# Normalised attention followed by a gated MLP: the first group in halves, the g product on GpSimd, and a newly searched plan

## The chip, the cores and the metric

The kernel runs on one core of a Trainium2 chip. The metric is the device time of one execution in microseconds (us); the kernel is run several times and the median counts. One more execution is recorded by the hardware profiler, and the views quoted below come from that one.

## The reference

The attention part normalises every row of q and k by its root mean square and multiplies it by g_q or g_k, takes a softmax, and multiplies by v. The MLP part takes the 12 heads side by side as rows of 768, applies a first matrix with a relu, normalises one half (v) over its 512 columns, mixes that half along the sequence with w_spatial, multiplies by the other half (u), and applies the last matrix.

```python
# q, k, v: (8, 12, 448, 64) float32; g_q, g_k: (64,)
q_n, k_n = x / sqrt(mean(x * x, -1) + 1e-6) * g   # for q with g_q, for k with g_k
attn = softmax(q_n @ k_n.T / sqrt(64))
x = (attn @ v) with the heads side by side         # (8, 448, 768)
h = relu(x @ w_in)                                 # w_in (768, 1024)
u, v = h[..., :512], h[..., 512:]
v_n = (v - mean(v)) / sqrt(var(v) + 1e-6)
gated = u * (w_spatial @ v_n + b_spatial)          # w_spatial (448, 448), along the sequence
out = gated @ w_out                                # w_out (512, 768)
```

## The kernel before

The work is cut into 24 groups G of four heads, three groups to each of the 8 batches b. For a group the program loads q and k (448 KB each, 128 partitions x 2 x 448 float32, two heads on each half of the middle axis), squares them (line 498 on ScalarE, line 500 on VectorE or GpSimd), reduces the squares to one number per row (513), turns that into 1/rms with a logarithm and an exponential on ScalarE (520, 524), scales the rows to bf16 (537), and turns the result so that the head dimension lies on the partitions. For the first six groups TensorE turns it (553) and VectorE or ScalarE copies it out of PSUM (562, 564, 566); later groups use a transposing DMA on the SP queue (575). The product g_q * g_k / 8, a column called `g2_col`, is multiplied into k in that copy. It comes from two small loads (357), a product of two rows on VectorE (401), a one-column matmul (408) and a copy (412).

A group then has seven rounds: four matmuls of scores (604, 64 x 64 tiles, two at a time in the array) and one exponential over 128 x 896 on ScalarE (628). The sums of the exponentials (652, a matmul with ones) and the values (676) follow, with a reciprocal by logarithm and exponential (660, 664) and the product with it (685). After three groups a batch has its x, and the MLP of that batch follows: the v half (718, 722), relu (693, 695), its statistics (742, 746), logarithm and exponential (752, 756) and application (764), the u half (776), the spatial mix (792) with the gating product (797), and the output matmuls (816, 837) with their copies (804, 806) and stores (828, 848).

None of this is written in loops that run on the chip. Every step is a `Task` with an estimated cost on each engine that could do it, a due position `pos`, its dependencies, and the buffers that it takes (`get`) or holds (`use`). `Planner.run` lays the tasks out on the five engines one by one in estimated time, picking by position, and emits each task's instructions as it is placed. Several tasks can go to more than one engine. The result is a fixed order of instructions on every engine; each engine runs its own list in order, and semaphores connect the lists. A dependency may be written as a pair (task, early), which lets the planner start the dependent that much before the estimated end of the task. The table `NUDGE` holds some hundreds of corrections to positions and engine choices, found by a search against the planner's own estimates.

Four more pieces matter here. The four TensorE modes "S", "V", "G" and "O" stand for shapes of the array, and the planner counts 0.095 us for each change of mode. `fill` puts dummy matmuls (371) into gaps of TensorE up to 25.5 us of planned time. `hold_back` ties a load to a compute instruction that ends about when the load should start. `hand_over` makes GpSimd wait for the VectorE instruction[...].

```python
    LOOK = {"PE": 0.3, "ACT": 0.9, "DVE": 1.1, "POOL": 0.6, "SP": 0.2}
    WAIT = 4.0
    SWITCH = 0.095
    KEEP = 0.6
```

## Time and profile before

| what | value |
|---|---|
| median of 5 runs | 279.21 us (275.97, 276.42, 279.21, 279.99, 281.34) |
| the profiled execution, its own time | 279.84 us |
| its span, first to last instruction | 277.9 us |
| TensorE (PE) busy | 261.4 us, 94% |
| ScalarE (ACT) busy | 216.6 us, 78% |
| VectorE (DVE) busy | 201.1 us, 72% |
| GpSimd (POOL) busy | 158.7 us, 57% |
| TensorE clock granted, mean | 0.985 |
| HBM read and written | 38.55 MB and 11.01 MB |

The span starts at the first instruction of any engine, and the time of an execution also has what lies around the span, here 279.84 - 277.9 = 1.9 us. The page gives for every group of instructions its line, engine, tiles, count and mean duration in ns. Two views give order in time: the timeline (start, duration, engine, line, and in brackets the idle time before it with what ended it) and the chain of waits that ended last, followed back from the last instruction. Ends of matmuls are modelled by the profiler, so "busy" on TensorE also holds part of the pipeline's fill.

### The profile page before, as it was taken

The page shows a single profiled execution, that of the slowest core. Times are in us where ns is not written, and L with a number is a line of the kernel's source. Part 1 is how long each engine was busy: PE and PEld are TensorE (multiplying, and loading weights), DVE is VectorE, ACT ScalarE, POOL GpSimd, SP SyncE. Part 2 cuts the span into 40 slices and gives each one's busy share as a digit, 9 for nine tenths or more (in the row PEclk, how much of TensorE's full clock was granted, in tenths as well). Part 3 has the DMA queues.
Part 4 walks back from the last instruction along what each step waited for, and adds up shares of the span by engine and source line. Part 5 has one row for each costly group of instructions (what it writes and reads, how often), then busy time and mean ns, then how long its engine had stood idle before and what let it go on. Part 6 is the DMA issues. An engine that isn't in the chain of part 4 may idle for free.

```text
span 277.9 us, 7116 instructions
## 1 busy us (share of the span) xinstructions
PE 261.4 (94%) x2850; PEld 126.8 (46%) x2859; DVE 201.1 (72%) x350; ACT 216.6 (78%) x353; POOL 158.7 (57%) x130
## 2 busy tenths in 40 slices
PE   5669899999999999999999999999999999999991
PEld 5434464444344354444544454544444444455440
DVE  4686899977888559887786868877887667554760
ACT  4387999978889889787898788869889877994321
POOL 7556274079788795998597874876987340000000
PEclk9978999999999999999999999999999999999998
DMA  7989669589799989999999989977899491015006
GB/s 246 286 190 232 158 152 241 159 186 192 189 256 226 159 226 220 251 178 222 286 139 231 198 219 250 213 189 163 268 216 120 92 207 36 0 28 160 15 19 180
DMA packets 65506, 50.01 MB, mean 180 GB/s; under 512 B 41985, under 2 KB 61954, under 8 KB 65474
## 3 DMA queue, kind: packets, MB, share of 16 engines
q1 hardware_dynamic: 51266, 40.61, 59.9%
q0 software_dynamic: 13888, 8.27, 22.4%
q10 hardware_dynamic: 320, 0.69, 0.7%
q8 instruction: 22, 0.36, 0.5%
q14 instruction: 10, 0.08, 0.1%
HBM read 38.55 MB, written 11.01 MB: 178 GB/s over the span
## 4 chain that ended last, share of the span: by engine, by line
PE 79%; ACT 6%; DMA 5%; DVE 2%; POOL 2%; issue 2%; SPq 1%; ACTq 0%
PE ps L776 13%; PE ps L676 12%; PE ps L604 12%; PE ps L718 11%; PE ps L816 10%; PE ps L792 8%; PE ps L652 7%; ACT et L628 5%; DMA qf<-in_q_dram 4%; PE ps L722 2%; PE ps L837 2%; DMA out_dram<-osb 1%; PE ps L553 1%; PE ps L463 1%; POOL sq L500 1%
## 5 line engine op out<-in xcount | busy, mean ns | idle before, releaser
L628 ACT ACTIVATE et<-ps 128x896 bf16<-128x896 f32 x168 | 144.8, 917 | 21.5 <-PE ps L604 20.9
L513 DVE TENSOR_REDUCE ms<-sq 128x14 f32<-128x896 f32 (+1 forms) x50 | 51.3, 1039 | 7.2 <-POOL sq L500 6.0
L604 PE MATMUL ps<-qT,kT 64*64 64x448 bf16 x672 | 47.4, 363 | 4.7 <-ACT et L628 3.8
L685 DVE TENSOR_TENSOR xt<-ps,rc 128x448 bf16<-128x448 f32 x48 | 28.3, 620 | 21.6 <-ACT rc L664 13.3
L500 POOL TENSOR_TENSOR sq<-kf 128x896 f32<-128x896 f32 x23 | 38.6, 1680 | 7.3 <-DVE nk L537 3.0
L676 PE MATMUL ps<-et,vt 128*32 128x448 bf16 x768 | 42.0, 354 | 0.0
L500 POOL TENSOR_TENSOR sq<-qf 128x896 f32<-128x896 f32 x19 | 32.0, 1683 | 14.4 <-issue 5.0
L776 PE MATMUL ps<-xt,w_in 128*128 128x448 bf16 x192 | 40.1, 353 | 0.0
L537 POOL TENSOR_TENSOR nq<-qf,rs 128x896 bf16<-128x896 f32 x18 | 30.5, 1692 | 12.3 <-issue 6.3
L537 POOL TENSOR_TENSOR nk<-kf,rs 128x896 bf16<-128x896 f32 x18 | 30.5, 1692 | 8.4 <-ACT rs L524 5.7
L816 PE MATMUL ps<-w_out,gt 128*128 128x384 bf16 x192 | 34.2, 327 | 0.2 <-DVE gt L797 0.2
L718 PE MATMUL ps<-w_in,xt 128*128 128x512 bf16 x135 | 33.4, 380 | 0.8 <-issue 0.3
L426 POOL DMA_DIRECT2D vt<-in_v_dram x32 | 21.6, 680 | 16.6 <-DVE us L695 7.7
L604 PEld LDWEIGHTS <-kT 64*64 64x64 bf16 x672 | 16.4, 105 | 30.7 <-issue 26.4
L676 PEld LDWEIGHTS <-vt 128*32 128x32 bf16 x768 | 19.7, 96 | 18.5 <-issue 6.1
L792 PE MATMUL ps<-w_spT,vn 128*128 128x448 bf16 (+1 forms) x128 | 27.0, 353 | 0.1
L776 PEld LDWEIGHTS <-w_in 128*128 128x128 bf16 x192 | 17.2, 98 | 20.8 <-issue 6.6
L797 DVE TENSOR_TENSOR gt<-ps,us 128x448 bf16<-128x448 f32 x32 | 19.5, 621 | 8.2 <-PE ps L792 7.0
L816 PEld LDWEIGHTS <-gt 128*128 128x128 bf16 x192 | 17.5, 98 | 15.9 <-issue 4.9
L742 DVE BATCH_NORM_STATS2 s<-vs 128x6 f32<-128x512 bf16 (+1 forms) x32 | 21.6, 685 | 4.0 <-ACT vs L693 3.6
L652 PE MATMUL ps<-et,ones 128*32 128x448 bf16 x384 | 23.7, 364 | 0.0
L804 ACT ACTIVATE osb<-ps 128x384 f32<-128x384 f32 x31 | 14.6, 491 | 11.2 <-PE ps L816 8.4
(68 smaller groups left out, 260.4 us busy)
## 6 DMA issues: line engine op xcount, KB each, us to landing
qf<-in_q_dram SPq DMA_DIRECT2D x24, 448.0 KB, 4.6
kf<-in_k_dram SPq DMA_DIRECT2D x24, 448.0 KB, 4.5
out_dram<-osb SPq DMA_DIRECT2D x45, 192.0 KB, 3.1
vt<-in_v_dram POOLq DMA_DIRECT2D x16, 192.0 KB, 6.2
vt<-in_v_dram POOLq DMA_DIRECT2D x16, 144.0 KB, 6.1
w_in<-in_moe_w_in_dram POOLq DMA_DIRECT2D x2, 768.0 KB, 7.5
out_dram<-osb SPq DMA_DIRECT2D x15, 96.0 KB, 3.6
w_out<-in_moe_w_out_dram POOLq DMA_DIRECT2D x1, 768.0 KB, 9.7
```

The lines of the kernel that those rows point to most:

```text
L500: eng_of[e].tensor_tensor(out=sqb.t[:, h], in0=r.t[:, h], in1=r.t[:, h], op=ALU.mult)
L513: dve.tensor_reduce(out=ms.t[:, i, h], in_=sqb.t[:, h].rearrange("p a (s d) -> p a s d", d=D), axis=AX.X, op=ALU.add)
L537: eng_of[e].tensor_tensor(out=nb.t.rearrange("p s a d -> p a s d")[:, :, s0:s1, :], in0=r.t.rearrange("p a (s d) -> p a s d", d=D)[:, :, s ...
L604: pe.matmul(out=ps[64 * h:64 * h + 64, a, 0:S], lhsT=kb[64 * a:64 * a + 64, slot, 64 * xk:64 * xk + 64], rhs=qb[64 * a:64 * a + 64, :, 64 ...
L628: act.activation(out=eb.t[:, r], in_=bf.t[:, :, 0:S], func=AF.Exp, bias=0.0, scale=1.0)
L652: pe.matmul(out=bf.t[32 * l:32 * l + 32, 0:S], lhsT=ones[:, (0 if c < 3 else 1 + x), :], rhs=eb.t[:, r, a, :], start=(c == 0), stop=(c == ...
L676: pe.matmul(out=bf.t[32 * l:32 * l + 32, 0:S], lhsT=vb.t[:, 2 * (g + 3 * a) + x, c, half::2], rhs=eb.t[:, r, a, :], start=(c == 0), stop=( ...
L685: dve.tensor_tensor(out=xb.t[:, j * S:j * S + S], in0=bf.t[:, 0:S], in1=rc.t, op=ALU.mult)
L718: pe.matmul(out=bf.t, lhsT=xb.t[:, j * S + 128 * c:j * S + 128 * c + 128], rhs=w_in[:, j, DH:DF], start=(j == 0), stop=(j == 5))
L776: pe.matmul(out=bf.t[:, 0:S], lhsT=w_in[:, j, 128 * f:128 * f + 128], rhs=xb.t[:, j * S:j * S + S], start=(j == 0), stop=(j == 5))
L792: pe.matmul(out=bf.t[:, 0:S], lhsT=vn.t[0:kp, c, 128 * f:128 * f + 128], rhs=w_spT[0:kp, c, :], start=(c == 0), stop=(c == 3))
L816: pe.matmul(out=bf.t[:, 0:384], lhsT=gt.t[:, f, 128 * c:128 * c + 128], rhs=w_out[:, f, 384 * h:384 * h + 384], start=(f == 0), stop=(f == 3))
```

## The change

Four things change.

- The first loads are cut. q and k of group 0 come in two DMAs each, one for each half of the middle axis, and each square waits for its own half. The logarithm and exponential of group 0 are done for q and for k apart, so the scaling of q waits for q's sums alone. Later groups keep one load and one pair.
- The product of the g rows becomes a plain product that may run on VectorE or GpSimd (it lands on GpSimd), and the factor 1/8 moves into the copy of the column, which may run on ScalarE (it does) or VectorE.
- In the planner, a sums, values or v-half matmul group that continues another one no longer waits for the estimated 0.26 us until that one's result is out: the dependency becomes (task, 0.26).
- The table `NUDGE` is replaced as a whole; it was searched in two stages. With it the order of the instructions on every engine and the engine of a number of tasks change through the whole program.

All that the program computes is the same. The diff, with the table cut:

```diff
--- before.py
+++ after.py
@@ -388,20 +388,22 @@
         b, g = divmod(G, NG)
         for i in range(2):
             bf = raw[G, i] = Buf(P_raw[i])
-
-            def emit(e, bf=bf, src=(q_x, k_x)[i][b][g]):
-                sync.dma_start(out=bf.t, in_=src)
-
-            raw_t[G, i] = [add(f"load{i} G{G}", {"SP": (0.6, 0)}, due(G) - 26 + i * 0.1, emit, get=[bf], dma=1.2 if G < 3 else 1.4,
-                               after=0.0 if G < 3 else (9.0, 20.0, 27.0)[G - 3] if G < 6 else due(G) - 26)]
+            raw_t[G, i] = []
+            for h in [slice(0, 1), slice(1, 2)] if G == 0 else [slice(0, 2)]:
+                def emit(e, bf=bf, h=h, src=(q_x, k_x)[i][b][g]):
+                    sync.dma_start(out=bf.t[:, h], in_=src[:, h])
+
+                raw_t[G, i].append(add(f"load{i} G{G}", {"SP": (0.6, 0)}, due(G) - 26 + i * 0.1 + 0.05 * h.start, emit,
+                                       get=[] if h.start else [bf], use=[bf] if h.start else [],
+                                       dma=0.6 if G == 0 else 1.2 if G < 3 else 1.4,
+                                       after=0.0 if G < 3 else (9.0, 20.0, 27.0)[G - 3] if G < 6 else due(G) - 26))
     g2_row = const.tile([1, 128], FP, name="g2_row")
     g2_col = const.tile([128, 1], FP, name="g2_col")
 
     def emit(e):
-        dve.scalar_tensor_tensor(out=g2_row, in0=g_row[:, 0].rearrange("o t d -> o (t d)"), scalar=scale,
-                                 in1=g_row[:, 1].rearrange("o t d -> o (t d)"),
-                                 op0=ALU.mult, op1=ALU.mult)
-    g_t = add("g2", {"DVE": (0.3, 0.3)}, 5.0, emit, after=7.0)
+        eng_of[e].tensor_tensor(out=g2_row, in0=g_row[:, 0].rearrange("o t d -> o (t d)"),
+                                in1=g_row[:, 1].rearrange("o t d -> o (t d)"), op=ALU.mult)
+    g_t = add("g2", {"DVE": (0.3, 0.3), "POOL": (0.35, 0.45)}, 5.0, emit, after=7.0)
     g_b = Buf(P_w)
 
     def emit(e):
@@ -409,8 +411,11 @@
     g_t = add("g2 col", {"PE": (0.1, 0.4)}, 5.0, emit, deps=[g_t], get=[g_b], mode="G")
 
     def emit(e):
-        dve.tensor_copy(out=g2_col, in_=g_b.t[:, 0:1])
-    g_t = add("g2 copy", {"DVE": (0.1, 0.2)}, 5.0, emit, deps=[g_t], use=[g_b])
+        if e == "ACT":
+            act.activation(out=g2_col, in_=g_b.t[:, 0:1], func=AF.Copy, bias=0.0, scale=scale)
+        else:
+            dve.tensor_scalar(out=g2_col, in0=g_b.t[:, 0:1], scalar1=scale, scalar2=None, op0=ALU.mult)
+    g_t = add("g2 copy", {"DVE": (0.1, 0.2), "ACT": (0.13, 0.25)}, 5.0, emit, deps=[g_t], use=[g_b])
 
     vb, v_t = {}, {}
     for b in range(B):
@@ -506,7 +511,7 @@
                     del costs["POOL"]
                 a = add(f"square{i} G{G} {j}", costs, d - (8 if early else 19) + 0.1 * i + 0.2 * j, emit, port=True,
                         bias={"ACT": 0.5 if G == 1 else 5.0} if G else None,
-                        deps=raw_t[G, i], get=[] if j else [sqb], use=[raw[G, i]] + ([sqb] if j else []))
+                        deps=[raw_t[G, i][j]], get=[] if j else [sqb], use=[raw[G, i]] + ([sqb] if j else []))
                 get, use = ms_use()
 
                 def emit(e, i=i, h=h, sqb=sqb, ms=ms_b):
@@ -516,13 +521,16 @@
                                   d - (7 if early else 17) + 0.1 * i + 0.2 * j, emit,
                                   deps=[a], get=get, use=[sqb] + use))
 
-        def emit(e, G=G, ms=ms_b):
-            act.activation(out=P_ln[G % 4], in_=ms.t, func=AF.Ln, bias=eps, scale=1.0 / D)
-        rs = add(f"rstd_ln G{G}", {"ACT": (0.13, 0.35)}, d - (6 if early else 15), emit, deps=red[0] + red[1], use=[ms_b])
-
-        def emit(e, G=G):
-            act.activation(out=P_rs[G % 4], in_=P_ln[G % 4], func=AF.Exp, bias=0.0, scale=-0.5)
-        rs = add(f"rstd G{G}", {"ACT": (0.13, 0.39)}, d - (6 if early else 15), emit, deps=[rs], use=[ms_b])
+        rs = []
+        for x in [slice(0, 1), slice(1, 2)] if G == 0 else [slice(0, 2)]:
+            def emit(e, G=G, ms=ms_b, x=x):
+                act.activation(out=P_ln[G % 4][:, x], in_=ms.t[:, x], func=AF.Ln, bias=eps, scale=1.0 / D)
+            ln = add(f"rstd_ln G{G}", {"ACT": (0.13, 0.35)}, d - (6 if early else 15), emit,
+                     deps=[t for y in range(x.start, x.stop) for t in red[y]], use=[ms_b])
+
+            def emit(e, G=G, x=x):
+                act.activation(out=P_rs[G % 4][:, x], in_=P_ln[G % 4][:, x], func=AF.Exp, bias=0.0, scale=-0.5)
+            rs.append(add(f"rstd G{G}", {"ACT": (0.13, 0.39)}, d - (6 if early else 15), emit, deps=[ln], use=[ms_b]))
         parts = []
         for i in range(2):
             tb = Buf(P_t[i])
@@ -545,7 +553,7 @@
                 if G == 0:
                     del costs["POOL"]
                 a = add(f"scaled{i} G{G} {n}", costs, d - (5 if early else 13) + 0.1 * i, emit, port=True,
-                        deps=[rs], get=[] if n else [nb], use=[raw[G, i], ms_b] + ([nb] if n else []))
+                        deps=[rs[-1 if G else i]], get=[] if n else [nb], use=[raw[G, i], ms_b] + ([nb] if n else []))
                 if G < PE_TURNED:
                     def emit(e, nb=nb, bf=bf, s0=s0, s1=s1):
                         ps = bf.t.bitcast(BF)
@@ -652,7 +660,7 @@
                         pe.matmul(out=bf.t[32 * l:32 * l + 32, 0:S], lhsT=ones[:, (0 if c < 3 else 1 + x), :],
                                   rhs=eb.t[:, r, a, :], start=(c == 0), stop=(c == 3), tile_position=(0, 32 * l))
             w = 0.1893 * (c1 - c0)
-            sm = add(f"sums G{G} {n}", {"PE": (w, w + 0.26)}, pos, emit, deps=need[n] + ([sm] if n else []),
+            sm = add(f"sums G{G} {n}", {"PE": (w, w + 0.26)}, pos, emit, deps=need[n] + ([(sm, 0.26)] if n else []),
                      get=[] if n else [bf], use=[eb] + ([bf] if n else []), mode="V")
         rc = Buf(P_rc)
 
@@ -678,7 +686,7 @@
                                       rhs=eb.t[:, r, a, :], start=(c == 0), stop=(c == 3), tile_position=(0, 32 * l))
                 w = 0.1893 * (c1 - c0)
                 a = add(f"values{half} G{G} {n}", {"PE": (w, w + 0.26)}, pos + 0.01 + 0.01 * half, emit,
-                        deps=need[n] + v_t[b] + ([a] if n else [sm] if len(cuts) == 1 else []),
+                        deps=need[n] + v_t[b] + ([(a, 0.26)] if n else [(sm, 0.26)] if len(cuts) == 1 else []),
                         get=[] if n else [bf], use=[eb, vb[b]] + ([bf] if n else []), mode="V")
 
             def emit(e, bf=bf, rc=rc, xb=xt_b[b], j=2 * g + half):
@@ -724,7 +732,7 @@
                                           tile_position=(0, 64 * h))
                 w = (1.3 if c < 3 else 0.66) / 6 * (j1 - j0)
                 a = add(f"unit_v{c} b{b} {j0}", {"PE": (w, w + 0.26)}, pos, emit,
-                        deps=[(x, w / (j1 - j0) * max(0, j - j0)) for j, x in enumerate(xts[:j1])] + w_t + ([a] if j0 else []),
+                        deps=[(x, w / (j1 - j0) * max(0, j - j0)) for j, x in enumerate(xts[:j1])] + w_t + ([(a, 0.26)] if j0 else []),
                         get=[] if j0 else [bf], use=[xb] + ([bf] if j0 else []), mode="G" if c < 3 else "O")
             n = 128 if c < 3 else 64
@@ -853,94 +861,88 @@
 LOG = None
 NUDGE = {
-    "load0 G1": 56, "load1 G3": -102, "load1 G7": -29, "load0 G9": 10, "load0 G10": -89, "load1 G10": -53,
...
+    "load1 G0 #2": -30, "load1 G6": -39, "load1 G13": -16, "load0 G14": 12, "load0 G16": 24, "g2 @DVE": 10,
...
 }
```

## The prediction

> **What bounds the kernel now.** I read the busy table and the slices of the page, then windows, then the timeline of the first 40 us, then the chain of waits.
>
> ```profile
> PE 261.4 (94%) x2850; PEld 126.8 (46%) x2859; DVE 201.1 (72%) x350; ACT 216.6 (78%) x353; POOL 158.7 (57%) x130
> ...
> PE   5669899999999999999999999999999999999991
> ...
> PEclk9978999999999999999999999999999999999998
> ```
>
> TensorE is full from slice 6 to the last but one. The windows (us; busy us of PE, PEld, DVE, ACT, POOL; clock; DMA) say from where:
>
> ```profile
> 18.00:20.00 2.00, 1.95 (x17) 0.96 (x15) 2.00 (x3) 2.00 (x3) 0.74 (x2) 0.50 1.01 198
> 36.00:40.00 4.00, 4.00 (x80) 3.38 (x76) 3.57 (x6) 3.96 (x6) 2.95 (x5) 1.00 0.30 38
> 40.00:60.00 20.00, 19.95 (x248) 9.32 (x247) 18.06 (x31) 18.90 (x32) 7.45 (x9) 1.00 0.86 191
> ```
>
> From 36 to 250 us TensorE is idle for 0.99 us in all (213.01 busy of 214, over six such windows). So the time is the head, until TensorE is full, plus a fixed amount of matmul work, plus the tail. In the head another engine sets the pace, as the timeline shows:
>
> ```profile
> 9.10 1.16 DVE L537 TENSOR_TENSOR nk<-kf,rs 128x512 bf16<-128x512 f32 x2
> 12.51 0.76 PE L604 MATMUL ps<-qT,kT 64*64 64x448 bf16 x12 [0.61 <-DVE qT L564]
> 14.44 0.95 ACT L498 ACTIVATE sq<-qf 128x896 f32<-128x896 f32 x1 [1.32 <-DMA qf<-in_q_dram]
> 15.29 1.70 ACT L628 ACTIVATE et<-ps 128x896 bf16<-128x896 f32 x2
> 16.24 0.38 PE L604 MATMUL ps<-qT,kT 64*64 64x448 bf16 x4 [2.53 <-ACT et L628]
> 22.16 1.62 PE L652 MATMUL ps<-et,ones 128*32 128x448 bf16 x16
> 24.28 0.91 ACT L628 ACTIVATE et<-ps 128x896 bf16<-128x896 f32 x1
> 33.09 6.56 ACT L628 ACTIVATE et<-ps 128x896 bf16<-128x896 f32 x8
> ```
>
> The first scores are ready by 12.9 us, but the first exponential starts at 15.29: ScalarE has the square of group 2's q ahead of it in its list, and that q lands at 14.44. TensorE then stands 2.53 us and its clock is halved (0.50 in the window 18 to 20), so the first sums take 1.62 us. ScalarE is close to full to 39.64, when nine exponentials of groups 2 and 3 are done. The chain of waits (start, duration, what) begins with that load; its later lines are blocks of matmuls whose lengths I use below:
>
> ```profile
> 3.33 11.09 DMA qf<-in_q_dram
> 14.44 0.95 ACT sq L498
> ...
> 56.01 0.50 PE ps L604 x8
> 56.52 1.24 PE ps L776 x6
> ...
> 87.14 2.38 PE ps L776 x12
> ...
> 101.38 0.69 PE ps L604 x12
> ```
>
> **What the Trainium skill says.** "TensorE: Matmul & The Clock Gate", section "Part 1: The HAM clock gate", says that the array runs at half rate after an idle window of about 3.4 us and that the window runs free of the program. The trace agrees: 2.53 us of idle, mostly in one such stretch, then 0.50. Since the window is free, other executions may have kept the clock; the spread 275.97 to 281.34 may hold this. The same page's table of specifications calls ScalarE's queue strict FIFO; the 2.4 us lost before 15.29 are that. "DMA: Bandwidth & Descriptors", section "Queues, rings and completion order", says that each DMA engine takes the queues it has work for in turn. The trace agrees: alone, loads land 1.2 us apart (4.40, 5.61); once v's four transfers on GpSimd's queue are in flight (issued 6.13 to 8.8), the third to sixth land at 7.3, 10.1, 12.2 and 14.4.
>
> **The change, part by part.** The places of the instructions are those of the built programs' lists and of the waits written in them; durations are from the rows above unless said.
>
> *Halves.* The first square starts at 4.40 now, when all of q is there. 448 KB take 1.2 us at the spacing above, so half of q may be there 0.6 us earlier, at 3.8. The four squares and four reductions (0.59 us each on VectorE, 2.36 for four) then end at about 6.8 instead of 7.37. Two more DMA issues of 0.5 us push the other loads' issues on SP back by 1.0 us; the transfers are queued behind each other by then, so I cost them at nothing (without that cover, 1.0). The extra pair of logarithm and exponential on 14 columns costs 0.55 us of ScalarE (0.32 + 0.23, the row with 28 columns), before 7.5 us, while nothing else of its list has landed.
>
> *The g product.* Now VectorE waits for g_k until 8.27, multiplies, waits for the matmul and copies to 9.18, with the scalings behind it. That goes: the scalings start at about 6.9 and, with 2.3 us for the four, end at 9.2 instead of 11.33. The product on GpSimd has no row for 1 x 128; VectorE's 0.28 is the low end, twice that the high end ("GPSIMD Engine Reference", section 3, has GpSimd about 2x slower; here 1.68 against 1.08 for 128 x 896). I take 0.35: after v's last issue, 8.8 to 9.15. GpSimd's next square waits for a load to 12.2 anyway. The one-column matmul stands on TensorE ahead of the last three turns of q and all of k, so these wait to 9.5 and are done by 10.3. The column's copy on ScalarE (0.16 to 0.3) sits before a load's wait and is hidden.
>
> *What is late next.* ScalarE's list is now: its three squares of group 0, two pairs of logarithm and exponential, square of group 1's q, the column, square of group 1's k, copy of k's first part, exponentials. The loads are reordered to q1, k1, q2, k2, so k1 is the fourth and should land where the fourth did, at 10.1. Then 0.95 (square) + 0.65 (copy of 512 columns) + 0.4 (k's second part on VectorE, which waits for the first) + 0.5 (scores) put the first exponential at 12.6. Before, it was the sixth load, and 15.29: 2.7 us gained. If k1 lands with 9.0 or 12.2 (bounds: k1 without most of the v traffic, and the fifth load's time), the gain is 3.8 or 0.6.
>
> *To the saturated stretch.* Group 0: two exponentials, logarithm and exponential, five more, at 0.82 each (6.56 for eight): done at 19.6. Turns of group 1 end before that. Sums 0.87 if the clock holds, reciprocal 1.1, and group 1's exponentials start at 21.7; before 24.28, one of them ahead of a 0.58 reciprocal. Seven take 5.8, the pair and the reciprocal of group 1 1.7: 29.3. Nine more take 7.4: 36.7 against 39.64. The head is shorter by 2.9, say 2.8. If the clock halves again, the turns cost 0.5 (1.61 for 14 against twice 0.56) and the sums 0.75 more: 1.5.
>
> *The searched plan.* Blocks of scores show the price of a change of mode: twelve matmuls 0.69, eight 0.50, so four cost 0.19 and each block 0.12 on top; the u half gives 1.24 for six and 2.38 for twelve, 0.10 on top. The order has 173 changes instead of 184, and from group 3's first scores on 154 instead of 164: 10 x 0.10 = 1.0 us less. The dropped 0.26 changes no instruction: TensorE never waited for its own continuation. The 15 dummies fewer lie in idle time. Five full squares fall to ScalarE instead of three and four output copies go from it to VectorE; both stay under TensorE.
>
> *Tail.* The last matmuls now are the narrow output block (0.77) and a 96 KB store instead of 192 KB (2.8 against 3.1 us to landing), and eight of batch 6's output matmuls lie between the last u half and the mix, where TensorE otherwise nears a wait. I take 0.2, bounds -0.5 and 0.7.
>
> *Sum.* 2.8 + 1.0 + 0.2 = 4.0. Against the profiled execution 279.84 - 4.0 = 275.8. That one lies 0.6 above the median of 279.21; one like the median would give 275.2. I take 275.5. No waits of the new plan inside 40 to 250 us are in the sum; bounds -0.5 (the 0.99 of now halves) and +4.
>
> **Rivals.** *The head gives all:* k1 lands at 9.0 and the clock holds, so 3.8 to 4 in the head, 1.0 in changes of mode, 0.7 in the tail, 0.4 fewer stalls: about 6.0, 273.5. For it: the halved clock came from a gap that the new list lacks. Against: v's transfers are issued when they were. *The load hides it:* k1 lands with 12.2, or the clock halves anyway; head 0.6, the rest 1.2, 278.0. For it: every load after the third was slow. *Slower:* the new plan stops TensorE in the saturated stretch. The place is groups 6 on, where q and k come through SP's list of loads, transposes and stores, each behind the one before. The price is 0.5 us a time, as the two stalls at 35.1 and 70.0 (0.6 and 0.5); over eight of them, 4.0 us, it decides, and with fifteen the time is 279.8 - 4.0 + 7.5 = 283.3. For it: the plan was fitted to estimates, and with less slack. Against: so was the old one, and it lost 0.99. *Nothing done:* the edit might do less than said, but the lists show the wait gone and the column moved.
>
> **How the numbers follow.** Likeliest 0.50 (275.5, from 274.2 to 277), head gives all 0.25, load hides it 0.15, slower 0.10. Two per cent, about what a measurement of this kernel can tell from no change, is 5.6 us: faster means under 273.6, slower over 284.8. Faster 0.25: about the second case. Slower 0.06: the far part of the last. Same 0.69. The range runs from 272.5 to 279.5; it takes in the bounds of k1's landing and of the tail and leaves the slower case out.
>
> **What would show it.** In the changed profile: first exponential near 12.6, right after k's copy, with k1's square before it ended by a load near 10; no VectorE wait on g; group 1's exponentials from about 21.7; nine of groups 2 and 3 done by 37; no window at 0.50 in 16 to 24; TensorE idle under 1.5 us from 36 to 250. Wrong: a first exponential after 14, a halved clock, or idle over 3 us in the long stretch.

## The result, and the profile after

The changed kernel takes 277.01 us (median of 44 runs, 275.87 to 279.57), the kernel before 276.32 us (79 runs beside it, 275.32 to 282.09). The ratio is 1.003, 95% interval [1.0016, 1.0044]: 0.7 us slower. I forecast 275.5 us, a gain of 4.0 us on the execution that I worked from. Times of one kernel differ by a few us between its executions, and that profiled execution (279.84 us), like three of the five times shown of before, was one of the long ones; what follows shows why this matters.

The page of the profiled execution of after (span 275.0 us, time 277.01 us), its busy row, TensorE's slices and the clock:

```profile
PE 260.1 (95%) x2834; PEld 126.6 (46%) x2844; DVE 202.1 (73%) x352; ACT 219.8 (80%) x353; POOL 157.9 (57%) x130
...
PE   5798999999999999989999999999999999999992
...
PEclk9889999999999999999999999999999999999999
```

The windows of after (columns as before: PE, PEld, DVE, ACT, POOL busy, clock, DMA share, GB/s). They cover the head's half clock and the long full stretch:

```profile
12.00:14.00 2.00, 1.94 (x17) 0.78 (x15) 2.00 (x3) 1.05 (x2) 1.48 (x3) 0.53 1.52 201
...
40.00:60.00 20.00, 19.58 (x226) 9.33 (x224) 17.65 (x32) 18.44 (x30) 8.80 (x8) 1.00 0.84 181
...
100.00:150.00 50.00, 48.75 (x530) 22.83 (x526) 38.76 (x71) 43.59 (x69) 36.89 (x28) 1.00 1.04 214
```

Over all windows from 36 to 250 us TensorE is busy for 211.33 of 214 us: 2.67 us idle, 0.99 before. The half clock has not gone; it lies at 12 to 15 us instead of 17 to 23. The timeline of the head of after, by start, duration, engine and line:

```profile
8.89 0.87 POOL L404 TENSOR_TENSOR g_row<-g_row 1x128 f32<-1x128 f32 x1
9.82 0.38 PE L410 MATMUL ps<-one_f,g_row 1*128 1x1 f32 x2 [0.88 <-POOL g_row L404]
10.23 0.17 ACT L415 ACTIVATE g_col<-ps 128x1 f32<-128x1 f32 x1 [1.01 <-PE ps L410]
10.30 0.94 ACT L503 ACTIVATE sq<-kf 128x896 f32<-128x896 f32 x1
11.14 0.68 ACT L570 ACTIVATE kT<-ps,g_col 128x512 bf16<-128x512 bf16 x1
11.87 1.78 PE L612 MATMUL ps<-qT,kT 64*64 64x448 bf16 x12 [0.85 <-ACT kT L570]
12.95 1.73 ACT L636 ACTIVATE et<-ps 128x896 bf16<-128x896 f32 x2 [1.13 <-PE ps L612]
...
20.61 5.78 ACT L636 ACTIVATE et<-ps 128x896 bf16<-128x896 f32 x7
...
27.93 7.48 ACT L636 ACTIVATE et<-ps 128x896 bf16<-128x896 f32 x9
```

The first exponential starts at 12.95 (before 15.29), group 1's at 20.61 (24.28), and the nine of groups 2 and 3 end at 35.41 (39.65). The head is 4.2 us shorter than the one from which I predicted, more than the 2.8 forecast, and yet the kernel is not faster than its predecessor usually is.

The largest new stall of the full stretch, again in the timeline of after:

```profile
118.95 1.68 POOL L505 TENSOR_TENSOR sq<-qf 128x896 f32<-128x896 f32 x1 [0.75 <-DMA qf<-in_q_dram]
...
120.67 1.09 DVE L518 TENSOR_REDUCE ms<-sq 128x14 f32<-128x896 f32 x1 [2.46 <-POOL sq L505]
121.67 1.15 DVE L693 TENSOR_TENSOR xt<-ps,rc 128x448 bf16<-128x448 f32 x2
122.34 0.38 PE L612 MATMUL ps<-qT,kT 64*64 64x448 bf16 x4 [0.89 <-DVE xt L693]
```

It reads backwards: TensorE's scores wait 0.89 us for VectorE to scale x; VectorE, in its list, has a reduction ahead of that, which waits for a square on GpSimd, which waited for a transfer of q issued at 112.17 and landed at 118.95.

### The profile page after: what moved, and what is told of

The parts are those of the page before. It is cut to its first block, busy times and chain, and to the rows that moved or that the text cites. A ratio compares the mean times of both kernels' runs of the same rounds, so it can differ in the third digit from the quotient of the medians.

```text
span 275.0 us, 7118 instructions
## 1 busy us (share of the span) xinstructions
PE 260.1 (95%) x2834; PEld 126.6 (46%) x2844; DVE 202.1 (73%) x352; ACT 219.8 (80%) x353; POOL 157.9 (57%) x130
## 5 line engine op out<-in xcount | busy, mean ns | idle before, releaser
L636 ACT ACTIVATE et<-ps 128x896 bf16<-128x896 f32 x168 | 143.8, 918 | 21.0 <-PE ps L612 20.4
L505 POOL TENSOR_TENSOR sq<-qf 128x896 f32<-128x896 f32 x20 | 33.6, 1679 | 18.9 <-DMA qf<-in_q_dram 11.2
L545 POOL TENSOR_TENSOR nq<-qf,rs 128x896 bf16<-128x896 f32 x19 | 32.3, 1700 | 19.2 <-ACT rs L532 8.1
L693 DVE TENSOR_TENSOR xt<-ps,rc 128x448 bf16<-128x448 f32 x48 | 28.2, 620 | 19.5 <-ACT rc L672 11.4
L505 POOL TENSOR_TENSOR sq<-kf 128x896 f32<-128x896 f32 x20 | 33.6, 1680 | 2.2 <-DMA kf<-in_k_dram 1.3
L431 POOL DMA_DIRECT2D vt<-in_v_dram x32 | 21.5, 675 | 18.3 <-ACT rs L532 10.2
L612 PEld LDWEIGHTS <-kT 64*64 64x64 bf16 x672 | 15.7, 105 | 29.5 <-issue 23.1
L684 PEld LDWEIGHTS <-vt 128*32 128x32 bf16 x768 | 20.5, 97 | 16.5 <-issue 3.2
L784 PEld LDWEIGHTS <-w_in 128*128 128x128 bf16 x192 | 17.3, 98 | 20.4 <-issue 6.4
L703 DVE TENSOR_SCALAR vs<-ps 64x256 bf16<-64x256 f32 (+1 forms) x28 | 15.5, 552 | 10.7 <-PE ps L730 5.9
```

The costliest lines, as they stand in the source:

```text
L505: eng_of[e].tensor_tensor(out=sqb.t[:, h], in0=r.t[:, h], in1=r.t[:, h], op=ALU.mult)
L545: eng_of[e].tensor_tensor(out=nb.t.rearrange("p s a d -> p a s d")[:, :, s0:s1, :], in0=r.t.rearrange("p a (s d) -> p a s d", d=D)[:, :, s ...
L612: pe.matmul(out=ps[64 * h:64 * h + 64, a, 0:S], lhsT=kb[64 * a:64 * a + 64, slot, 64 * xk:64 * xk + 64], rhs=qb[64 * a:64 * a + 64, :, 64 ...
L636: act.activation(out=eb.t[:, r], in_=bf.t[:, :, 0:S], func=AF.Exp, bias=0.0, scale=1.0)
L684: pe.matmul(out=bf.t[32 * l:32 * l + 32, 0:S], lhsT=vb.t[:, 2 * (g + 3 * a) + x, c, half::2], rhs=eb.t[:, r, a, :], start=(c == 0), stop=( ...
L693: dve.tensor_tensor(out=xb.t[:, j * S:j * S + S], in0=bf.t[:, 0:S], in1=rc.t, op=ALU.mult)
```

## The experiments

The theories at the start were: A, the profiled execution of before was an unusual one, a usual head of before is some 3 us shorter, so that the head gains little and the new plan loses that and more later; B, the head gains 3 to 4 us every time, and later waits take it back; C, the head's edits do nothing. After the first results came D: the head's edits themselves cost; and, for the halves alone, E: they cost through later stalls and not in the head. Where a kernel below is said to follow an order "written out", the planner's search is replaced by the finished list of tasks, so that one task can be moved and nothing else.

**Before, once more** (`before_again`, and later `before_3`; no edit).

> The kernel before, unchanged, for a second profile of its head. Theory A (the execution profiled first was not a typical one): the sixth load lands near 12.5 us instead of 14.4, the first exponential starts before 13.8 instead of 15.3, no window has the clock at 0.50, and the nine exponentials of groups 2 and 3 are done by 37 instead of 39.6; time near 276.3. Theory B (the head is always like that, and the changed kernel gains 3 to 4 us there and loses it later): first exponential at 15 to 15.5, nine done at 39 to 40.

It took 276.91 us, with a span of 275.0, the very span of after. ScalarE in its timeline:

```profile
13.07 0.95 ACT L498 ACTIVATE sq<-qf 128x896 f32<-128x896 f32 x1 [0.49 <-DMA qf<-in_q_dram]
...
30.20 6.56 ACT L628 ACTIVATE et<-ps 128x896 bf16<-128x896 f32 x8
```

The sixth load, on which ScalarE's square waits, is there at 13.07, not 14.44; the first exponential starts at 13.92; the clock stays at 1.00 in every window to 36 us; the nine exponentials end at 36.76. That is 2.9 us ahead of the first profile, and the time is 2.9 us shorter. The stretched blocks of scores further on return at the same distance (they start at 67.1 for 70.0 and at 175.3 for 178.3). This supports A. A third profile was taken at the end:

> A third profile of the kernel before, for its usual head: at its median of 276.1 to 276.3 us the nine exponentials of groups 2 and 3 should be done at 36.0 to 36.2 if the rest is as fixed as it was (240.1), and not at 39.64 as in the execution from which I predicted.

275.72 us. ScalarE's timeline in it:

```profile
11.01 1.79 ACT L566 ACTIVATE sq<-qf 128x896 f32<-128x896 f32 x2
...
28.98 6.56 ACT L696 ACTIVATE et<-ps 128x896 bf16<-128x896 f32 x8
```

Here both squares run without a wait; the sixth load has landed at 10.6. The first exponential starts at 12.69, earlier than in after, with the old order of loads. VectorE doesn't wait for the g rows either: it waited for g_k for 0.91 us in the first profile of before and for 0.55 in `before_again`, and here only for the one-column matmul (0.78). The nine end at 35.54.

**The blocked square moved** (`unblocked`): before's order, with the square of group 2's q behind the first two exponentials.

```diff
 ScalarE:  square q G1
-          square q G2
           exp G0 r0, exp G0 r1
+          square q G2
```

> The kernel before with one move in its order: ScalarE's square of group 2's q, which waits for the sixth load, stands behind the first two exponentials instead of ahead of them. Theory A: in most executions that load has landed or nearly so, so little changes: ratio 0.996 to 1.000, and what is gained lies in the executions over 278. Theory B: 0.988 to 0.992.

276.45 us, ratio 1.0007 [0.9989, 1.0025]. By the times, the move brings nothing that can be told from before, so the wait that I had called the 2.4 us lost costs little in most executions. Its profile can't show more: the sixth load landed at 10.6 there too, so the square would not have waited. The first exponential starts at 12.83 and the nine end at 36.62, while in `before_3`, with the square in front, they end at 35.54. That something behind the wait hides it, such as VectorE's reductions and scalings of group 1, is a guess.

**Heads exchanged** (`head_new`, `head_old`): the order of after up to group 3's first exponential and then the order of before for what is left, and the reverse.

```diff
-order = after
+order = after[:first exp of G3] + [task for task in before if not yet placed]
```

> The changed kernel's code and its order of instructions up to the first exponential of group 3, then the order of the kernel before for all that is left. Theory A: the head's gain in a typical execution is 0.5 to 1.2 us, and the old order behind it adds nothing: ratio to before 0.995 to 0.998. Theory B: ratio 0.985 to 0.989 (272.2 to 273.3). A third theory (C), that the halves and the moved product give nothing at all: 0.999 to 1.002.

> The mirror of the run above: the code and order of the kernel before up to the first exponential of group 3, then the changed kernel's order. Theory A: it loses the new order's stalls (idle of TensorE from 36 to 250 us of 2.7 instead of 1.0 us) without the head's gain: ratio 1.004 to 1.009. Theory B: 1.012 to 1.018. Theory C: as the changed kernel, 1.002 to 1.004.

299.93 us (ratio 1.0839 [1.0783, 1.0894]) and 293.86 us (1.0639 [1.0586, 1.0692]): no theory expected this. The nine exponentials are done at 36.9 and 36.2, so the heads are as they should be; the loss lies behind them. TensorE's waits in `head_new` are spread over many causes:

```profile
PE ps L866 <- DVE gt L871: 3.4, 4, 1.3
...
PE ps L534 <- ACT rc L734: 1.9, 1, 1.9
```

Each line gives what TensorE waited for, the sum in us, the number of waits and the longest. Two finished orders could not be sewn together here; that buffers and the lists of the five engines no longer meet is my reading of these waits. The experiment says nothing on A or B, and the parts had to be undone inside one order.

**The stall at 121 us** (`swap`): in after's order one reduction goes behind the scalings that it held up.

```diff
 VectorE:
-  reduce q squares G14
   xt0 G10, xt1 G10
+  reduce q squares G14
```

> The kernel after, with one instruction moved: VectorE's reduction of group 14's q squares goes behind the two scalings of x of group 10, which it holds up near 121 us in the profile of after (TensorE stands 1.24 us there, until one of these scalings frees its PSUM). Theory A (a typical execution of before already had most of the head's gain, and the new plan loses about 2.3 us of TensorE time between 36 and 250 us that the old one does not): the stall goes and stays gone, 0.8 to 1.2 us less, about 276.0 against 277.0, ratio to before about 0.999, and TensorE idle between 36 and 250 about 1.6 instead of 2.67. Theory B (the head gains 3 to 4 us in every execution and later waits take all of it back): the same direction, but TensorE then stops elsewhere, less than 0.4 gained. Theory C (the stalls are not on the path, only the amount of matmul work is): no change, 277.0.

276.85 us, ratio 1.0023 [1.0001, 1.0045], not told apart from after. The profiled execution was far from this median (280.76 us), so only its order of events is read: the same scaling still waits, now for its other input.

```profile
124.88 0.63 DVE L761 TENSOR_TENSOR xt<-ps,rc 128x448 bf16<-128x448 f32 x1 [2.39 <-ACT rc L740]
```

From 100 to 150 us TensorE was idle for 0.75 us instead of 1.25 in after. But from 36 to 250 us it was idle for 1.86, where the unchanged order (`after_again`, below) has 1.93: other waits came in place of this one. The 0.8 to 1.2 us that A expected did not come.

**Dummies for the clock** (`busy`): 18 more dummy matmuls in the two gaps of the head.

```diff
+8 dummies before the one-column matmul of g
+10 dummies before the first scores of group 0
```

> The kernel after, with 18 more of the dummy matmuls that keep TensorE's clock up: eight before the one-column matmul of g (its wait of 0.88 us near 9 us) and ten before the first scores (1.0 us near 11). They compute nothing that is used. If the halved clock between about 11.9 and 15 us in the profile of after is paid for, the first scores take 0.76 instead of 1.78 us, the first exponential starts near 12.0 instead of 12.95 and 0.5 to 0.9 us reach the end: 276.2 to 276.5. If VectorE's reductions and scalings of group 1 bind behind it, the first exponential moves but the end does not: 276.9 to 277.1.

276.38 us, ratio 1.0013 [0.9986, 1.0039]. The mean clock was under 0.993 in 4 of 15 executions; in after it was in 37 of 44. The time is in the expected 276.2 to 276.5, but the interval holds after's ratio of 1.003, so a gain is not shown. Its profiled execution, at 281.76 us, shows another way in which an execution gets long:

```profile
28.09 1.68 POOL L573 TENSOR_TENSOR sq<-kf 128x896 f32<-128x896 f32 x1 [2.91 <-DMA kf<-in_k_dram]
```

The head starts well (first exponential at 12.57), and then k of group 3 lands at 28.0 and VectorE's reduction waits 4.57 us for the square; in `both`, below, that square starts at 21.56. The long execution of `swap` has the same late load: the square starts at 26.70, after a wait of 3.83 us.

**The halves undone, and the GpSimd product undone** (`whole`, `gvec`).

```diff
-for h in [slice(0, 1), slice(1, 2)] if G == 0 else [slice(0, 2)]:   # loads
+for h in [slice(0, 2)]:                                            # whole only
```

```diff
 VectorE:  scale q G0
+          g2 = g_q * g_k          (was GpSimd's)      # gvec only
           scale k G0
 TensorE:  turns of q G0 (all seven), one-column matmul, turns of k G0
```

> The kernel after with one part undone: q and k of the first group are loaded in one transfer each again instead of in halves; every other instruction of every engine is where it was (four dummies more at the start). The first square starts near 4.2 instead of 3.43. All theories agree that little is lost, since the scalings wait behind the pair of logarithm and exponential: my steps gave the halves 0.5 us at most; Theory A: 0 to 0.5 us more, 277.0 to 277.5, theory C: 277.0 exactly. A gain (below 276.7) would say that the two added issues on SP cost more than the halves bring.

> The kernel after, with the product of the g rows back on VectorE, but between the scalings of q and of k, and the one-column matmul behind all turns of q: no 0.87 us GpSimd product in front of TensorE. In the profile of after TensorE waits 0.88 us for that product near 9 us and then runs the first scores at half clock (1.78 instead of 0.76 us). Theory A: the first exponential is still held by ScalarE's square of k1 and the copy of k behind it, so it moves only by what the clock gives: 12.95 to 11.9 if the clock is not halved, and at most 0.6 us of it reach the end (276.4 to 277.0). Theory B: the GpSimd product is the main loss of the head, 1.0 us or more at the end (276.0 or less).

`whole`: 275.89 us, ratio 0.9976 [0.9952, 1.0000]. `gvec`: 276.24 us, ratio 0.9991 [0.9965, 1.0018]. Undoing the halves helps: the interval lies clear below after's [1.0016, 1.0044]. This is the opposite of what I had priced, and against theory A's 277.0 or more. Undoing the GpSimd product points the same way, but its interval just reaches after's. The profiled execution of `whole` was its longest of 14 (277.22), so its trace doesn't show where the gain lies. This is where D came from, and it asked for after in the same series, for both undone, and for each edit alone on before.

**After again, and both undone** (`after_again`: after's order unchanged; `both`: the two diffs above together).

> The kernel after once more (its instructions written out from the same order), beside its own variants and on the same chip as they: the single undoing of the halved loads gave 275.9 (ratio 0.998 to before), that of the GpSimd product 276.2 (0.999), and the base for both has to be timed with them. Theory A (the head edits are worth about 1 us and the new plan loses more): 277.0, ratio 1.003. Theory D (the head edits themselves cost, through the order in which transfers land and the halved clock, and the new plan is worth a little): also 277.0. If it comes out at 276.2 or less (ratio below 1.001), the base moves from one chip or hour to another, and neither undoing is shown to bring anything.

> The new plan with both head edits taken back: q and k of the first group loaded in one transfer each, and the product of the g rows on VectorE between the scalings of q and k; the rest of the order of after is kept. Theory A: the undone edits were worth something, so 277 or more (ratio 1.003 or above). Theory D: their costs add up, 275.0 to 275.8 (ratio 0.995 to 0.998), and this beats both kernels.

`after_again` 277.17 us, ratio 1.0019 [0.9991, 1.0047]; `both` 275.25 us, ratio 0.9985 [0.9961, 1.0009]. `both` lies 1.9 us below after, timed beside it, and 0.8 below before's median there (276.05), though its interval against before still holds 1. The time is in D's range, the ratio is not (0.995 to 0.998 was expected). That the two costs add up is not shown: in medians the undoings bring 1.1 and 0.8 us alone and 1.9 together, but by the ratios 0.0054 and 0.0039 alone and 0.0034 together. ScalarE's timeline in `both`:

```profile
5.49 1.04 ACT L571 ACTIVATE sq<-kf 128x448 f32<-128x448 f32 x2 [0.63 <-DMA kf<-in_k_dram]
...
9.05 0.17 ACT L483 ACTIVATE g_col<-ps 128x1 f32<-128x1 f32 x1 [0.39 <-PE ps L478]
9.12 0.94 ACT L571 ACTIVATE sq<-kf 128x896 f32<-128x896 f32 x1
...
11.68 1.73 ACT L704 ACTIVATE et<-ps 128x896 bf16<-128x896 f32 x2 [0.92 <-PE ps L680]
...
26.75 7.48 ACT L704 ACTIVATE et<-ps 128x896 bf16<-128x896 f32 x9
```

and in `after_again`:

```profile
5.64 1.18 ACT L571 ACTIVATE sq<-kf 128x448 f32<-128x448 f32 x2 [1.11 <-DMA kf<-in_k_dram]
...
9.92 0.17 ACT L483 ACTIVATE g_col<-ps 128x1 f32<-128x1 f32 x1 [1.02 <-PE ps L478]
9.98 0.94 ACT L571 ACTIVATE sq<-kf 128x896 f32<-128x896 f32 x1
```

The square of k1 follows the column copy without a wait for its load in both kernels. So k1 had landed before 9.12 in `both` and before 9.98 in `after_again`, where ScalarE had stood 1.0 us for the column in front of it.

**Each edit alone on before** (`bhalves`: the loads in halves, each square waiting for its half; `bgpool`: the product on GpSimd, the one-column matmul behind the turns of k, the column copied by ScalarE).

> The kernel before with the halved loads alone: q and k of the first group in two transfers each, every square waiting for its own half, nothing else moved. Theory A: the scalings of the first group still wait for the g rows near 8 us, so nothing is gained or lost: ratio 1.000 within 0.002. Theory D: two more transfers ahead of the others in the queues put the later loads back, 0.4 to 1.0 us more (ratio 1.002 to 1.004).

> The kernel before with the product of the g rows on GpSimd alone (behind v's four issues), the one-column matmul behind the turns of k, and the scaled column copied by ScalarE; the scalings no longer wait for the g rows. The product of 0.87 us ends near 9.8 us, so the copy of k that needs the column starts near 10.5, as it does already (10.58). Theory A: no more than 0.3 us either way, ratio 0.999 to 1.001. Theory D: the gap on TensorE in front of the one-column matmul halves its clock in more executions, 0.3 to 1.0 us more, ratio 1.001 to 1.004.

`bhalves`: 277.74 us, ratio 1.0036 [1.001, 1.0063]: the halves cost here too, with no other edit beside them. `bgpool`: 275.67 us, ratio 0.9984 [0.9945, 1.0023]: nothing that can be told from before. The profiled execution of `bhalves` was its fastest (275.84); two more were profiled:

> A second profile of the kernel before with the halved loads alone. Theory D (the halves put later transfers back): in an execution near its median of 277.7 us, one of the loads of groups 1 to 3 lands 1 to 3 us later than in the fast one (there the exponentials of groups 2 and 3 were done at 35.82), they are done at 37.6, and the end still follows 240.1 us later with 0.3 us of TensorE idle between 36 and 250. Theory E (stalls later on): done by 36, and over 1.5 us idle.

> A third profile of the same kernel, for the spread between executions: theory D expects another landing order and again the end 240.1 us after the last of the nine exponentials; theory E expects idle time of TensorE between 36 and 250 us that differs from one execution to the next.

277.96 and 276.53 us. The nine exponentials end at 37.88 and 36.50, as theory D's rule requires; TensorE is idle for 0.35 and 0.34 us from 36 to 250, which ends theory E for the old plan. In `bhalves_2` ScalarE's timeline has

```profile
10.23 1.16 ACT L633 ACTIVATE kT<-ps,g_col 128x512 bf16<-128x512 bf16 x2 [1.75 <-PE ps L624]
...
13.11 0.95 ACT L569 ACTIVATE sq<-qf 128x896 f32<-128x896 f32 x1 [0.87 <-DMA qf<-in_q_dram]
```

and its clock is 0.50 from 14.3 to 21.1 us; in `bhalves_3` it is so from 12.2 to 15.6. The copy of k, the first line, starts at 9.80, 10.23 and 10.40 in the three profiles with halves, and at 9.96, 10.58 and 10.70 in those of before. So in these profiles group 0 is not later through the halves in the old plan; what they cost there comes after it.

## Why the prediction was wrong, and where it was right

Two rules come out of the profiles. The first: in the old plan the end follows the nine exponentials of groups 2 and 3 at a fixed distance, whatever made them late. In the new plan the distance is longer, and differs; `busy` and `swap`, which keep after's order but for dummies or one reduction, have another one than after.

| execution | first exponential | nine exponentials done | time | time less done |
|---|---|---|---|---|
| before, as first profiled | 15.29 | 39.65 | 279.84 | 240.2 |
| before_again | 13.92 | 36.76 | 276.91 | 240.2 |
| before_3 | 12.69 | 35.54 | 275.72 | 240.2 |
| unblocked | 12.83 | 36.62 | 276.62 | 240.0 |
| bgpool | 14.27 | 38.68 | 278.66 | 240.0 |
| bhalves | 12.53 | 35.82 | 275.84 | 240.0 |
| bhalves_2 | 13.96 | 37.88 | 277.96 | 240.1 |
| bhalves_3 | 13.13 | 36.50 | 276.53 | 240.0 |
| after | 12.95 | 35.41 | 277.01 | 241.6 |
| after_again | 12.43 | 35.40 | 277.00 | 241.6 |
| gvec | 13.12 | 36.15 | 276.77 | 240.6 |
| whole | 12.58 | 36.56 | 277.22 | 240.7 |
| both | 11.68 | 34.23 | 275.05 | 240.8 |
| swap | 12.94 | 39.69 | 280.76 | 241.1 |
| busy | 12.57 | 40.72 | 281.76 | 241.0 |

The second uses TensorE's matmuls alone. I give each its usual interval to the next one (189 ns for one of the u half, some 47 ns for one of the scores, where four share the array), add these up to the work done so far, and call the start time less that sum the lag. From 20 us of work (near 43 us) to 222 us of work, close to the end, the lag grows by 19.5 us in all seven profiles of old-plan kernels whose trace is complete (they agree within 0.02), by 20.2 in `both` and `whole`, by 20.4 in `gvec` and by 21.2 in `after_again`.

Now the steps of the prediction. Two of them carry the error. The forecast was a gain of 4.0 us, the result is a loss of 0.7: 4.7 apart. The head was taken from an unusual execution, which makes 2.0 of it. The rest lies behind the head: 1.2 was counted as gained there (mode changes and tail), and by the table 1.4 was lost (241.6 less 240.2), which makes 2.6. Within the head the halves and the column were mis-priced as well.

*The base.* "The sum is made against its own time", and the head that I shortened was an unusual one. By the first rule before's median of 276.32 belongs to a head that ends at 36.2, not 39.65. The prediction did say that other executions might have kept the clock, but put it into the range, not into the base. Against 36.2, after's 35.4 is 0.8 us gained, where I counted 2.8. "The load hides it" named a head of 0.6, near this size, but gave it 0.15 and put a gain of 1.2 behind it.

*Halves.* Forecast: first square 0.6 us earlier, the four reductions done 0.57 earlier, two more issues on SP "at nothing (without that cover, 1.0)". The first half did come early (3.43). But k's second half is the fourth issue instead of the second. The timeline of SP's issues in `before_3` and after:

```profile
1.26 1.47 SPq L461 DMA_DIRECT2D kf<-in_k_dram  x3
```

```profile
1.67 0.91 SPq L394 DMA_DIRECT2D kf<-in_k_dram  x2
```

Three issues take 1.47 us, so k of group 0 as a whole is issued by about 1.75 in `before_3`; in after the second half of k is issued by 2.58, some 0.8 later. The last square of k ends at 6.44 to 6.65 in the eight profiled executions with whole loads, and at 6.79 to 7.82 in the nine with halves: 0.7 later on the mean, where I had 0.57 earlier. So this term failed: the cover was missing for the very transfers that had been split. By the times the halves cost 1.1 us in the new plan (`whole`) and 1.7 in the old one (`bhalves`), where I had named 1.0 as the price without cover; how much of it goes through the last square stays open: in the old plan the copy of k is no later in the profiles. What the traces show besides is the fourth load. With whole loads it landed at 7.9 to 8.8 in four profiles and at 9.5 to 10.1 in the other four; with halves, issued 0.8 later, at 8.5 to 10.0, never as early as 7.9. "DMA: Bandwidth & Descriptors" of the Trainium skill, section "Issuing engines are not separate DMA queues", says that the time of an initiation is usually small relative to the transfer; here an issue takes 0.46 us and a half of q or k, by the 1.2 us spacing, about 0.6, so that it is not small.

*The g product.* VectorE's stall went as forecast: its four scalings end at 10.2, in the first profile of before at 11.3; in `before_3` they end at 10.6, so that a usual execution gains less. GpSimd's product took 0.48 to 0.87 us in seven profiles, 0.87 in after, where my high end was 0.56 and my value 0.35. "GPSIMD Engine Reference" of the Trainium skill, section 3.1 ("Elementwise — side-by-side cycle accounting"), has 2.6 cycles an element on GpSimd, by which 128 elements alone come to an estimate of 0.28 us at the page's 1.2 GHz; its 156 ns for dispatch stand under VectorE, and it gives no number for GpSimd's. All seven are above that estimate, and I had scaled VectorE's time instead. The product began at 8.89, when v's last issue was done, so the column came to ScalarE at 10.23. "The column's copy ... sits before a load's wait and is hidden" is the second term of the head that failed. ScalarE's list stood 1.0 us for the column with k1's square and the copy of k behind it, and in `both`, where the column is early, k1 is there before 9.12. With the product on VectorE and the loads whole the first exponential starts at 11.68, 0.75 ahead of `after_again`. On before alone the same move cost nothing that can be told (`bgpool`). There the copy of k is next behind the column: it starts at 10.38, and in the three profiles of before, where it waits for the turns, at 9.96 to 10.70.

*What is late next; the clock.* The first exponential, 12.6 forecast, came at 12.95 and 12.43: right, but with luck, since not k1 but the column set it. k1 had landed by 9.2 and 9.8, the forecast said 10.1. Group 1's exponentials came at 20.6 (forecast 21.7), the nine at 35.4 (36.7). Part of this is an addition of mine: 12.6, seven exponentials of 0.82 and a pair of 0.55 make 18.9, not 19.6. The wide spacing of the third to sixth load, which I put down to v's transfers taking turns with them, is not fixed by these: in `before_3` v is issued at the same time, but the fourth to sixth load land at 8.0, 9.2 and 10.6, and the first of v at 11.3. What decides between the two stays open. The halved clock did not go away. Its mean was under 0.993 in 43 of 144 timed executions of before, 56 of 66 of after, 15 of 22 of `bhalves`, 10 of 14 of `whole` and 3 of 22 of `both`. It costs the first scores of after 0.6 us: 1.78, against the same twelve in `after_again`, where the clock is 1.00:

```profile
11.56 1.21 PE L680 MATMUL ps<-qT,kT 64*64 64x448 bf16 x12 [0.85 <-ACT kT L638]
```

Only 0.2 us of this reach the first exponential (1.08 us after the scores' start in after, 0.87 in `after_again`). In after the executions with the lower clock are no slower (277.02 against 277.01 in the median; in `after_again` 277.35 against 276.32, of three). In before they are: 279.03 against 275.84 in the 67 timed last, and 277.81 against 276.57 in `bhalves`; whether the clock or the late load that goes with it makes them long isn't separated. Its part in the 0.7 us stays open, and `busy`, with few such executions, isn't told apart from after. I had also taken the trace of before to agree with an idle window of 3.4 us. The stretches at half clock do last 3.4 us or twice that in these traces, but no such stretch was idle before them: the longest idle time of TensorE just ahead was 2.53 us in before and 0.88 in after.

*Mode changes.* From 20 us of work on `after_again` has 149 blocks of one mode and `before_3` 157, each with about 0.12 us of its own: 1.0 us less, as the step said.

*Waits of the new plan.* "No waits of the new plan inside 40 to 250 us are in the sum": this term failed, and it is the larger of the two that carry the error. The pauses beyond that 0.12, as far as longer than 0.15 us, come to 1.6 us in `before_3`, 3.6 in `after_again` and 2.6 in `both`, and shorter ones add 0.5 more in both new-plan kernels. The largest is the one near 121 us, 1.3 in `after_again` and 0.5 in `both`. In the windows from 36 to 250 us TensorE is idle for 0.34 us in `before_3`, 1.93 in `after_again`, 1.07 in `both`. So the new plan gives back more than the mode changes bring: some 0.7 us net in its best case (20.2 less 19.5) and 1.7 in `after_again`. The slower rival named this mechanism and its carrier, the chain of q and k through the queue, but priced it at eight stalls of 0.5; one stall of 1.2 us and a few small ones were enough to use up the gain in the head. (Of the two stalls that its price rests on, the trace has none of 0.6 us at 35.1; such an idle time of TensorE, 0.62 us, ends at 34.04, ahead of the full stretch.)

*Tail.* From the last matmul to the end of the time 7.7 us in `after_again`, 7.9 in `before_3`: 0.2, as said.

The sum, `after_again` less `before_3`, both profiled: the lag at 20 us of work is nearly the same (22.77 and 22.80), the long stretch costs 1.64, the matmuls at its end and the tail give 0.33 back: 1.3 us, which is 277.00 - 275.72. Against before's median, whose head is about 0.6 us later than that of `before_3` (276.32 less 275.72), 0.7 us is left, the measured difference.

**Shown and not shown.** That the halves cost is shown twice in times, by undoing them (`whole`) and alone (`bhalves`); the path is not. That the GpSimd product holds up the first exponential is shown by the traces of `after_again` and `both`, and that it costs time only together with the halves. That the edits cost in the head alone is not shown for the new plan, where E was not tested. Of the 1.95 us between the profiles of `after_again` and `both`, 1.2 lie up to the nine exponentials (35.40 to 34.23) and 0.8 behind them (241.6 to 240.8). In `whole` and `gvec` the nine end later than in after and the distance is shorter by 0.9 and 1.0, so there the later stall may well be most of what the undoing brings. What remains of the stall at 121 us without both edits (0.23 us idle from 100 to 150 in `both`) I can trace to the q transfer of 6.8 us that took under 6 there; why that transfer is faster, with TensorE then further ahead than in after, stays open. So does which landing is late in the long executions of the halves: `bhalves_2` shows a late sixth load and a halved clock together, as the first profile of before does.

## What to carry to other kernels

Before pricing a head that waits for transfers, profile it more than once: the wait that ends last in one execution may be absent in the next, and the base must be the usual execution. Splitting a transfer to start sooner can delay its last byte by the added issues (the last square ended 0.7 us later here), so look at what the consumer needs before it can go on; here all four squares were needed. Waits that a new plan brings belong in the sum with a price of their own, even when the old plan had next to none. And an instruction that "sits before a load's wait" is hidden only as long as the load is late; ask what stands behind it in its list once the load is early.

## What the runs showed of the hardware that was not expected

A product of 1 x 128 on GpSimd took 0.48, 0.53, 0.54, 0.62, 0.69, 0.85 and 0.87 us in seven profiles of the same instruction; on VectorE 0.27 and 0.28. VectorE's two scalings of k, which ran beside it, took 1.41 us in after and `after_again`, and 1.14 in `both`. The sixth load of before landed at 10.6, 13.0 and 14.4 in three executions of one program, and the time followed it: 275.72, 276.91, 279.84 us. TensorE's clock was halved without a wholly idle stretch of the length of the halving: in after for 3.4 us from 12.1, with idle times of 0.88 and 0.85 us in the 3.4 us before.
